# Laying the two blocks of a tile of query rows on alternate partitions instead of in halves

## The chip, the cores and the metric

The kernel runs on one core of one Trainium2 chip. The metric is the device time of one launch in microseconds. Three timed runs of the kernel before gave 817.63, 816.74 and 815.66 us: a median of 816.74 us. One further execution was profiled; everything that is read from the trace below comes from that one. The changed kernel computes the same output; only the place of rows in the on-chip memory and the order in which the host packs the query rows differ.

## The reference

Three layers run one after the other: attention with a position bias, a two-layer network, and a soft mixture of 8 experts.

```python
# attention: batch 4, 8 heads, 576 positions, 64 wide
scores = q @ k.T / 8
x    = log1p(|i - j|) / log1p(max(i, 1))         # i: query row, j: key row
bias = relu(x[..., None] @ w1 + b1) @ w2         # one 576 x 576 table per head
attn = softmax(scores + bias);  y = attn @ v     # -> 2304 tokens x 512
# network
h = y @ w_in                                     # 512 -> 2048
y = (max(h, 0) + alpha * min(h, 0)) @ w_out
# soft mixture: 32 slots, 4 for each of 8 experts
d = softmax(y @ phi, axis=0);  c = softmax(y @ phi, axis=1)
slots = d.T @ y
out   = c @ [relu(slots_e @ w1_e) @ w2_e  for each expert e]
```

The bias depends on the position and the head, not on the batch. So the kernel makes the bias table once, keeps it in device memory, and reads it back for each pair of heads.

## The kernel before, in words

**Blocks and tiles of query rows.** The 576 query rows are nine blocks of 64. Eight of them are paired to four tiles of 128 rows: tile c holds block c and block 8 - c, for c from 0 to 3. Block 4 is alone. In the kernel before, a tile's first block lies on partitions 0 to 63 and its second on partitions 64 to 127. The list `ROWS` on the host (L1281) says in which order the rows are packed, `_constants` (L1284) gives the positions of the rows of each tile in the same order, and `kernel` puts the output rows back into place with it (L1373).

**The bias phase (`bias_phase`, the first 77 us).** For nine groups k of 16 steps it makes step masks on ScalarE and VectorE (L142, L144), multiplies them on TensorE into sums `acc` (L160), and combines these on VectorE to bias rows (`tmp` L189, `rows` L193, L191), for the four tiles and for block 4. GpSimd writes the same values a second time, reversed, beside the first (L211), so that a row of the table holds the bias for all distances. When some columns of a tile are complete, `flush` sends them to device memory by `put` (L220), which calls `send` (L215): one DMA for the first block of the tile (`half` 0) and one for the second (`half` 1), each from 64 partitions (`q`, L222) to the tensor `W`, or to `W4` for block 4. Typical is one store of 64 rows x 4 head pairs x 1024 bytes, 256 KB. For head pairs 1 to 3 some stores are put off to the end of the phase (`late`).

**Attention (`Attention`).** It goes through 16 pairs of a head pair `hp` and a batch `b`, four batches to each head pair. For a head pair, the tile `nb` holds the bias of all its query rows. `bias_rows` (L324) fills it from `W` and `W4`: for each of the four 128-row tiles one read for the first block and one for the second, each of 64 rows into 64 partitions. For head pair 0 these are issued tile by tile (`bias_first`, L347), 288 KB a read, as early as the stores allow; for head pairs 1 to 3 all four tiles go in one read of 1152 KB a block, with two reads of 144 KB for block 4 (L345). For each pair and each of nine tiles: `scores` makes `s` on TensorE (L414), `least` subtracts the bias and takes the row's extreme on VectorE (`z`, `m`, L437), `power` takes the exponential on ScalarE (`e`, L457), `transposes` and `gather` turn it (`t` L477, `g` L491 and L493), and `pv` multiplies with the values (`o`, L505 and L510). Before the scores of a pair, GpSimd splits its inputs `raw` into high and low parts (`qh`, `kh` L382; `ql`, `kl` L384).

**What sets the order.** All DMAs around the change are issued by SyncE's queue, in program order from the late part of the bias phase on (`keep_in_program_order`). They go round eight completion semaphores: a DMA waits until the DMA issued eight before it has landed. In attention, the list `ROUND` (L299) fixes the order of the steps on the engines, with the scores of the next pair begun before the last pair is done. GpSimd also prepares inputs `x` of the network while attention runs (`xu` L634), from attention results that were stored to device memory (`xT` L518, `rs` L533 and L534) and read back (`xu` L619, `xb` L623). The network follows (`h` L725, `ys` L753), and then the experts (`hps` and `ops` L1136), with two steps around their start that the prediction names: `turn` (L1114), which a copy turns into `sst` (L1106 on ScalarE, L1108 on VectorE), and `tc` (L932), which turns the combine weights `cs` for the output.

Of the kernel before, what the change touches and what calls it, by code (L numbers as in the profile page):

```python
# [19 lines left out]
P = 128  # L20
B, H, S, D = 4, 8, 576, 64
# [48 lines left out]
def bias_phase(tc, ident, W, W4, cpack, lcol, prow, xmain, xtail, att):  # L70
# [3 lines left out]
    with ExitStack() as ctx:  # L74
# [73 lines left out]
        def unit(k, c):  # L148
# [4 lines left out]
            if c < 4:  # L153
                m, cols, dst = P, slice(P * c, P * c + P), acc
            else:
                m, cols = 64 * (k % 2) + 64, slice(512, S)
                dst = acc[m - 64 : m]
# [44 lines left out]
            a = both[:m, :, :, w + one - f0 - 64 : w + one - f0 - z]  # L202
            if c == 4:
                a, src = a[:, :, 0], fwd[:, :, 0]
# [10 lines left out]
            def send(dst, src, pin):  # L215
                i = nc.sync.dma_start(dst, src)
                if pin:
                    tc.keep_in_program_order(i)

            def put(half, blk, d0, n_r, n_l, one, hs):  # L220

                q = slice(64 * half, 64 * half + 64)  # L222
                if blk == 4:
                    e, dst = 1, W4.rearrange("h p j -> p h j")
                else:
                    e = 2
                    dst = W[blk - (blk > 4) if blk > 4 else 3 - blk, hs].rearrange("a p j b -> p a (j b)")
                src = mine.rearrange("p (h x) -> p h x", h=H // e)[:, hs if e == 2 else slice(0, H)]

                def move(j0, x0, n):  # L230
                    send(dst[:, :, e * j0 : e * (j0 + n)], src[q, :, e * x0 : e * (x0 + n)], k > 4)

                if one:
                    move(S - n_l, w - n_l + 1, n_l + n_r - 1)
                    return
                if n_r > 0:
                    move(S - 1 + d0, w, n_r)
                if n_l > 0:
                    y = int(d0 == 0)
                    move(S - d0 - n_l, w - n_l, n_l - y)  # L240

            def flush(hs):
                if c == 4:
                    for half in range(m // 64):
                        put(half, 4, d0 + 64 * half, 64, 64, False, hs)
                else:
                    far, near = min(w, S - 64 * c - d0), max(0, min(w, 64 * c + 64 - d0))
                    put(0, c, d0, far, near, one, hs)
                    put(1, 8 - c, d0, near, far, one, hs)
# [38 lines left out]
class Attention:  # L288
# [35 lines left out]
    def bias_rows(self, hp, s, n):  # L324

        nb = self.nb[hp]
        if s == 4:
            parts = [(64 * par, 4) for par in range(2)]
        else:
            parts = [(64 * q, s + 5 * q) for q in range(2)]  # L330
        for p0, blk in parts:
            i0 = 64 * (blk if blk >= 4 else 3 - blk)
            if s == 4:
                a = self.W4[2 * hp + p0 // 64, :, S - 1 - i0 : 2 * S - 1 - i0]
                src = bass.AP(tensor=a.tensor, offset=a.offset, ap=[[PITCH - 1, 64], [1, S]])
                dst = nb[p0 : p0 + 64, 8 * S :]
            else:
                a = self.W[blk - (blk > 4), hp, :, S - 1 - i0 : 2 * S - 1 - i0]
                step = H * 64 * PITCH + (128 if blk < 4 else -128)
                dims = [[2 * (PITCH - 1), 64], [step, n], [1, 2 * S]]  # L340
                src = bass.AP(tensor=a.tensor, offset=a.offset, ap=[d for d in dims if d[1] > 1])
                dst = nb[p0 : p0 + 64, 2 * S * s : 2 * S * (s + n)]
                if n > 1:
                    dst = dst.rearrange("p (s x) -> p s x", s=n)
            i = self.nc.sync.dma_start(dst, src)  # L345
            if hp == 0:
                self.tc.keep_in_program_order(i)  # L347
# [930 lines left out]

ROWS = [64 * blk + r for blk in (3, 5, 2, 6, 1, 7, 0, 8, 4) for r in range(64)]  # L1281


def _constants():  # L1284
    import numpy as np

    pos = np.arange(S)
    ld = np.log1p(pos.astype(np.float32))
    pi = np.log1p(np.maximum(pos.astype(np.float32), 1.0))
    x = (ld[None, :] / pi[:, None]).astype(np.float32)  # L1290
    lcol = np.repeat(ld.reshape(NTQ, 4).T, HID, axis=0)
    tiles = [np.r_[64 * c : 64 * c + 64, 64 * (8 - c) : 64 * (8 - c) + 64] for c in range(4)]
    up = (1 + np.maximum(pos, 1)).astype(np.float16)
    prow = np.tile(up[np.concatenate(tiles + [np.arange(256, 320)])][None, :], (P, 1))
    xmain = np.stack([x[r].reshape(P, NG, 64) for r in tiles], axis=2)
    mid = x[256:320]
    xtail = np.zeros((P, 3, 64), np.float32)
    for q in range(3):
        xtail[:64, q] = mid[:, 128 * q : 128 * q + 64]
        if q < 2:  # L1300
            xtail[64:, q] = mid[:, 128 * q + 64 : 128 * q + 128]

    row = np.arange(P).reshape(4, 2, 4, SPE)
    scon = np.zeros((P, P + 1), np.float32)
    for a in range(4):
        scon[row[:, :, 0], row[:, :, a]] = 1.0
    scon[row[:, :, 1::2].ravel(), P] = -1.0
    return dict(lcol=lcol, prow=prow, xmain=xmain, xtail=xtail, scon=scon)


def _layout(i):
    import numpy as np

    q = i["q"][:, :, ROWS].reshape(B, HP, 2, S, D).transpose(1, 0, 4, 2, 3)
    k = i["k"].reshape(B, HP, 2, S, D).transpose(1, 0, 4, 2, 3)
# [59 lines left out]
```

## Time and profile before

| | |
|---|---|
| median of three timed runs | 816.74 us (815.66 to 817.63) |
| the profiled execution: its own time | 816.62 us |
| the profiled execution: span of its instructions | 814.7 us |
| mean granted TensorE clock | 0.978 of full |
| TensorE matmul busy | 762.4 us (94%) |
| VectorE / ScalarE / GpSimd busy | 549.3 / 495.9 / 315.8 us |
| device memory read / written | 91.95 MB / 21.29 MB |

The span is what the trace covers; the execution's own time holds 1.9 us more around it. TensorE is the busy engine on the whole, but not in each stage: the bias phase and the start of attention have idle stretches of TensorE. [...]

### The profile page before, as it was taken

Reading aid. Unit: us, or ns where it says so; the run is one execution under the profiler, and the core shown is the slowest. Engines: PE = TensorE matmul, PEld = TensorE weight load, DVE = VectorE, ACT = ScalarE, POOL = GpSimd, SP = SyncE. Lnnn points to the kernel's source line nnn. Section 1 sums busy time; section 2 is a strip of 40 time slices with the busy share of each in tenths; the row PEclk is TensorE's granted clock in tenths of the full one; section 3 lists DMA queues with packets and bytes.
Section 4 is the critical chain, followed back from the end, with each engine's and each line's share of the span. In section 5 each row is a group of like instructions: output and inputs, shape, how many; then the busy total and the mean of one; then the engine's idle time right before and its main releaser. Section 6 shows DMA issues by size and latency. Waiting matters only on the chain.

```text
span 814.7 us, 18357 instructions
## 1 busy us (share of the span) xinstructions
PE 762.4 (94%) x7428; PEld 636.9 (78%) x7428; DVE 549.3 (67%) x958; ACT 495.9 (61%) x974; POOL 315.8 (39%) x239
## 2 busy tenths in 40 slices
PE   6886798999999999999999999999999999998993
PEld 6776676787877778988898989888888899886341
DVE  8887686888888856777778555655675756465103
ACT  8972787888888854444356566656566556655002
POOL 4633147275575713113224454445543641141000
PEclk9999799999999999999999999999999999999997
DMA  6598996748744542333340001401100124338996
GB/s 198 131 234 189 303 229 188 211 128 246 220 140 143 157 125 94 123 136 104 104 130 1 1 30 36 142 1 40 39 1 20 39 92 139 107 104 312 385 365 232
DMA packets 49670, 114.43 MB, mean 140 GB/s; under 512 B 10546, under 2 KB 29874, under 8 KB 47538
## 3 DMA queue, kind: packets, MB, share of 16 engines
q1 hardware_dynamic: 49584, 113.26, 44.7%
q8 instruction: 58, 0.95, 0.5%
q14 instruction: 28, 0.21, 0.1%
HBM read 91.95 MB, written 21.29 MB: 139 GB/s over the span
## 4 chain that ended last, share of the span: by engine, by line
PE 45%; DVE 3%; ACT 1%; DMA 1%; POOL 1%; issue 1%; DVEq 0%; ACTq 0%
PE h L725 18%; PE ys L753 18%; PE ops L1136 2%; PE hps L1136 2%; PE lp L823 1%; DMA em<-in_mw_dram 1%; PE turn L1145 1%; DVE x L644 0%; DVE g L736 0%; PE sp L882 0%; PE sp L883 0%; DVE wr L685 0%; DVE gr L741 0%; PE tl L870 0%; POOL w12l L714 0%
## 5 line engine op out<-in xcount | busy, mean ns | idle before, releaser
L736 DVE SCALAR_TENSOR_TENSOR g<-g,nal 128x384 f32<-128x384 f32 x96 | 100.9, 1051 | 84.0 <-ACT g L735 83.6
L437 DVE CUSTOM_DVE_ANT_0 z<-s,nb 128x576 f32<-128x576 f32 x144 | 108.3, 755 | 22.9 <-PE s L414 12.0
L457 ACT ACTIVATE e<-z,m 128x576 f32<-128x576 f32 x144 | 109.9, 767 | 6.7 <-DVE m L437 6.7
L739 ACT ACTIVATE gr<-g 128x384 fp32r<-128x384 f32 x96 | 50.2, 523 | 86.8 <-DVE g L736 86.6
L493 ACT ACTIVATE g<-t 128x640 f32<-128x640 f32 x96 | 67.3, 703 | 34.1 <-PE t L477 30.1
L505 PE MATMUL o<-g,v 128*64 128x256 f32 (+1 forms) x640 | 86.1, 414 | 0.5 <-ACT g L493 0.5
L733 ACT ACTIVATE g<-h 128x384 f32<-128x384 f32 x96 | 46.9, 489 | 54.4 <-PE h L725 50.1
L741 DVE TENSOR_TENSOR gr<-g,gr 128x384 fp32r<-128x384 f32 x80 | 53.6, 670 | 33.2 <-ACT gr L739 33.2
L477 PE MATMUL t<-ident,e 64*128 64x64 f32 x1440 | 69.1, 225 | 4.8 <-DVE m L437 2.9
L160 PE MATMUL acc<-wp,mask 128*128 128x64 bf16 (+1 forms) x1680 | 57.3, 198 | 16.9 <-issue 6.5
L477 PEld LDWEIGHTS t<-ident,e 64*128 64x128 f32 x1440 | 66.7, 141 | 6.7 <-issue 4.2
L160 PEld LDWEIGHTS <-mask 128*128 128x128 bf16 (+1 forms) x1680 | 55.2, 103 | 18.9 <-issue 7.5
L414 PE MATMUL s<-kh,qh 64*128 64x288 f32 x320 | 62.1, 384 | 4.7 <-DVE m L437 3.9
L505 PEld LDWEIGHTS o<-g,v 128*64 128x64 f32 x640 | 43.7, 138 | 29.0 <-ACT g L493 1.0
L142 ACT ACTIVATE mask<-pr,wb 128x576 bf16<-128x576 f16 (+4 forms) x94 | 54.9, 671 | 8.3 <-PE acc L160 8.3
L414 PE MATMUL s<-kl,qh 64*128 64x288 f32 x320 | 48.6, 299 | 2.6 <-POOL kl L384 2.6
L741 POOL TENSOR_TENSOR gr<-g,gr 128x384 fp32r<-128x384 f32 x16 | 19.4, 1212 | 77.7 <-issue 28.2
L414 PE MATMUL s<-kh,ql 64*128 64x288 f32 x320 | 48.6, 299 | 0.0
L382 POOL TENSOR_SCALAR qh<-raw 128x1216 fp32r<-128x1216 f32 x16 | 19.4, 1210 | 70.7 <-DMA raw<-in_qk_dram 49.5
L735 ACT ACTIVATE g<-h 128x384 f32<-128x384 f32 x96 | 46.5, 484 | 0.0
L384 POOL TENSOR_TENSOR ql<-raw,qh 128x1216 fp32r<-128x1216 f32 x16 | 45.2, 2827 | 0.0
L414 PEld LDWEIGHTS s<-kh,qh 64*128 64x128 f32 x320 | 31.5, 192 | 13.5 <-DVE m L437 4.4
(990 smaller groups left out, 2016.1 us busy)
## 6 DMA issues: line engine op xcount, KB each, us to landing
wide<-in_w_dram SPq DMA_DIRECT2D x16, 1024.0 KB
ep<-in_mw_dram SPq DMA_DIRECT2D x29, 512.0 KB
raw<-in_qk_dram SPq DMA_DIRECT2D x16, 896.0 KB
nb<-W SPq DMA_DIRECT2D x6, 1152.0 KB
v<-in_v_l_dram SPq DMA_DIRECT2D x16, 320.0 KB
pre<-in_mw_dram SPq DMA_DIRECT2D x10, 512.0 KB
ex<-in_mw_dram SPq DMA_DIRECT2D x9, 512.0 KB
em<-in_mw_dram SPq DMA_DIRECT2D x8, 512.0 KB
```

The lines of the kernel that those rows point to most:

```text
L142: nc.scalar.activation(dst, pr[:, :n], AF.Sigmoid, bias=wb[:, t : t + 1], scale=BIG)
L160: nc.tensor.matmul(dst[:, u // 8, :, :, 4 * (u % 8) : 4 * (u % 8) + 4], mask[:, (16 * k + u) % RING, cols], wp[:, part], start=part == 0, ...
L414: nc.tensor.matmul(s[:, hf, :288], st["q", a][d, o : o + P], st["k", b][d, 288 * h : 288 * h + 288], start=n_ == 0, stop=n_ == len(seq) - 1,),
L437: self.nc.vector.tensor_tensor_reduce(out=z.rearrange("p (a b) -> p a b", a=2), in0=s[:, :, :288], in1=nb.rearrange("p (a b) -> p a b", a= ...
L457: self.nc.scalar.activation(e, z, AF.Exp, bias=m, scale=-1.0, accum_out=st["sum"][:, slot : slot + 1]),
L477: self.pin(i, nc.tensor.transpose(tp[:, r, 64 * c : 64 * c + 64], e[q, k0 : k0 + P], self.ident[q, q]))
L493: self.pin(i, nc.scalar.activation(dst, src, AF.Copy))
L505: nc.tensor.matmul(op[64 * h : 64 * h + 64, 0, :n], st["v"][:, h, c], g[:, h, c], start=c == 0, stop=c == 4),
L725: nc.tensor.matmul(h, w_[:, c * P : (c + 1) * P], x_[:, c], start=c == 0 and n_ == 0, stop=c == NC - 1 and n_ == 2,)
L736: nc.vector.scalar_tensor_tensor(g, neg, self.nal[:, f : f + 1], g, ALU.mult, ALU.add)
L741: eng.tensor_tensor(gl, g, gh.bitcast(F32), ALU.subtract)
L753: i = self.nc.tensor.matmul(self.ys[blk][t], g_[:, t * P : (t + 1) * P], w_[:, 512:], start=f == 0 and n_ == 0, stop=f == NF - 1 and n_ == 2,)
```

## The change

A tile's first block now lies on the even partitions and its second block on the odd ones. On the host, `ROWS` and the position lists take rows of the two blocks in turn. In the kernel, `put` and `bias_rows` address partitions `half, half + 2, ...` in steps of two (`slice(half, P, 2)`, `slice(q, P, 2)`) in place of 64 neighbouring ones. Block 4 keeps its halves, in stores and in reads. Each DMA still moves 64 rows with the same bytes from and to the same addresses in device memory.

```diff
             def put(half, blk, d0, n_r, n_l, one, hs):
-                q = slice(64 * half, 64 * half + 64)
+                q = slice(64 * half, 64 * half + 64) if blk == 4 else slice(half, P, 2)
...
         if s == 4:
-            parts = [(64 * par, 4) for par in range(2)]
+            parts = [(slice(64 * par, 64 * par + 64), 4) for par in range(2)]
         else:
-            parts = [(64 * q, s + 5 * q) for q in range(2)]
-        for p0, blk in parts:
+            parts = [(slice(q, P, 2), s + 5 * q) for q in range(2)]
+        for p, blk in parts:
...
-                dst = nb[p0 : p0 + 64, 8 * S :]
+                dst = nb[p, 8 * S :]
...
-                dst = nb[p0 : p0 + 64, 2 * S * s : 2 * S * (s + n)]
+                dst = nb[p, 2 * S * s : 2 * S * (s + n)]
...
-ROWS = [64 * blk + r for blk in (3, 5, 2, 6, 1, 7, 0, 8, 4) for r in range(64)]
+ROWS = [64 * blk + r for n in (3, 2, 1, 0) for r in range(64) for blk in (n, 8 - n)] + list(range(256, 320))
...
-    tiles = [np.r_[64 * c : 64 * c + 64, 64 * (8 - c) : 64 * (8 - c) + 64] for c in range(4)]
+    tiles = [ROWS[P * (3 - c) : P * (4 - c)] for c in range(4)]
```

The instructions of SyncE and GpSimd stand in the same order before and after. The program is laid out by a scheduler, and it moves a few steps at the start of the experts. On TensorE, behind the eight products `turn`, the products `tc` stood ahead of the first `hps`, and now stand among them (the tile names are those of the section on the kernel; `pre`, `ep` and `et` are expert weights):

```order
-L932 MATMUL tc_0_10783<-ident,cs_0_10780 128x128 x2
 L1136 MATMUL hps<-pre,sst 32x512 x10
 L1136 MATMUL hps<-ep_9926,sst 32x512 x2
 L1136 MATMUL hps<-ep_9959,sst 32x512 x2
-L1136 MATMUL hps<-ep_10016,sst 32x512 x2
-L932 MATMUL tc_2_10798<-ident,cs_2_10795 128x128
+L1136 MATMUL hps<-ep_10016,sst 32x512
+L932 MATMUL tc_0_10783<-ident,cs_0_10780 128x128 x2
+L1136 MATMUL hps<-ep_10016,sst 32x512
```

Two products of `tc` have moved behind fifteen of the products of `hps`. On ScalarE at the same place, one copy of `turn` to `sst` and one exponential `c` change places:

```order
 L915 ACTIVATE c_0_10684<-c_0_10684 128x64
+L1106 ACTIVATE sst<-turn_10765 128x16x4
 L915 ACTIVATE c_2_10697<-c_2_10697 128x32
-L1106 ACTIVATE sst<-turn_10765 128x16x4
```

The copy to `sst`, for which the first `hps` waits, now stands one instruction earlier.

## Rows read from the trace of the kernel before

**Rows 1.** Busy time by stretch, with the columns' names; five stretches of the span.
```profile
core 0: us, PE busy (x) PEld busy (x) DVE busy (x) ACT busy (x) POOL busy (x), PEclk, DMA share, GB/s
...
76.00:98.00 22.00, 13.51 (x149) 11.13 (x148) 11.10 (x29) 12.48 (x27) 0.67 (x1) 0.69 0.98 271
...
133.00:142.00 9.00, 6.44 (x80) 4.91 (x76) 4.84 (x12) 5.13 (x11) 8.97 (x6) 0.81 0.75 181
142.00:290.00 148.00, 147.87 (x2187) 117.11 (x2185) 128.26 (x304) 124.41 (x270) 82.60 (x63) 1.00 0.59 176
290.00:740.00 450.00, 444.88 (x2457) 392.14 (x2452) 291.40 (x373) 251.31 (x468) 167.04 (x97) 1.00 0.23 75
740.00:814.60 74.60, 56.28 (x376) 27.98 (x375) 19.53 (x50) 15.53 (x38) 2.64 (x5) 0.90 0.88 333
```

**Rows 2.** Waits of the engines from 76 to 98 us: total, times, longest.
```profile
DVE z L437 <- DMA nb<-W: 8.0, 3, 3.9
...
PE s L414 <- DVE m L437: 3.9, 1, 3.9
```

**Rows 3.** Instructions in order of time, 73 to 87 us: start, duration, wait.
```profile
73.62 3.60 SPq L345 DMA_DIRECT2D nb<-W  x4
...
79.85 0.76 DVE L437 CUSTOM_DVE_ANT_0 z<-s,nb 128x576 f32<-128x576 f32 x1 [3.85 <-DMA nb<-W]
...
84.11 0.76 DVE L437 CUSTOM_DVE_ANT_0 z<-s,nb 128x576 f32<-128x576 f32 x1 [2.81 <-DMA nb<-W]
...
86.89 0.76 DVE L437 CUSTOM_DVE_ANT_0 z<-s,nb 128x576 f32<-128x576 f32 x1 [1.34 <-DMA nb<-W]
```

**Rows 4.** Instructions in order of time, 96 to 137 us, on SyncE, GpSimd and TensorE.
```profile
96.39 2.79 SPq L345 DMA_DIRECT2D nb<-W  x4
...
118.38 0.24 SPq L533 DMA_DIRECT2D rs<-rt  x1
...
126.99 1.01 POOL L634 TENSOR_TENSOR xu<-xu,xb 128x384 f32<-128x384 f32 x1 [13.64 <-DMA rs<-rt]
...
136.09 0.40 PE L414 MATMUL s<-kl,qh 64*128 64x288 f32 x2 [2.56 <-POOL kl L384]
```

**Rows 5.** Waits of SyncE's queue from 98 to 142 us: total, times, longest.
```profile
SPq L533 <- DMA nb<-W: 5.5, 1, 5.5
SPq L534 <- DMA nb<-W: 4.9, 1, 4.9
```

**Rows 6.** Busy time by stretch: loads of 128 rows, then two 64-row reads.
```profile
191.00:196.00 5.00, 5.00 (x82) 3.98 (x78) 4.28 (x13) 4.53 (x11) 5.00 (x4) 1.00 1.01 397
198.00:202.00 4.00, 4.00 (x41) 2.32 (x41) 2.90 (x7) 3.59 (x10) 0.00 (x0) 1.00 1.01 208
202.00:203.00 1.00, 1.00 (x22) 1.00 (x22) 0.96 (x3) 0.20 (x1) 0.58 (x1) 1.00 1.03 233
203.00:208.00 5.00, 5.00 (x76) 3.93 (x74) 4.61 (x12) 4.83 (x11) 5.00 (x4) 1.00 1.02 210
```

**Rows 7.** Busy time by stretch: the start of attention.
```profile
76.00:80.00 4.00, 0.81 (x11) 0.49 (x8) 0.15 (x1) 0.00 (x0) 0.67 (x1) 0.93 0.95 238
80.00:93.00 13.00, 8.85 (x86) 7.84 (x88) 7.86 (x20) 8.67 (x19) 0.00 (x0) 0.50 0.98 265
```

**Rows 8.** Busy time by stretch: the stores of the bias phase.
```profile
33.00:62.00 29.00, 25.22 (x753) 24.12 (x750) 23.07 (x46) 23.34 (x42) 9.86 (x15) 0.96 0.93 224
62.00:69.00 7.00, 5.04 (x168) 4.87 (x166) 6.50 (x16) 4.37 (x13) 2.24 (x3) 1.00 0.96 196
69.00:71.50 2.50, 2.50 (x93) 2.50 (x89) 2.50 (x6) 0.00 (x0) 1.00 (x2) 1.00 0.96 261
71.50:73.50 2.00, 1.35 (x47) 1.23 (x44) 1.49 (x4) 0.00 (x0) 0.95 (x2) 1.00 0.23 58
```

**Rows 9.** TensorE in order of time, start of the experts.
```profile
755.61 0.67 PE L932 MATMUL tc<-ident,cs 128*128 128x128 f32 x2
...
756.21 3.57 PE L1136 MATMUL hps<-pre,sst 128*32 128x512 f32 x17
```

More of the change, by code (lines that the diff above doesn't have):

```diff
@@ L327, in bias_rows @@
         if s == 4:
-            parts = [(64 * par, 4) for par in range(2)]
+            parts = [(slice(64 * par, 64 * par + 64), 4) for par in range(2)]
         else:
-            parts = [(64 * q, s + 5 * q) for q in range(2)]
-        for p0, blk in parts:
+            parts = [(slice(q, P, 2), s + 5 * q) for q in range(2)]
+        for p, blk in parts:
             i0 = 64 * (blk if blk >= 4 else 3 - blk)
             if s == 4:
-                a = self.W4[2 * hp + p0 // 64, :, S - 1 - i0 : 2 * S - 1 - i0]
+                a = self.W4[2 * hp + p.start // 64, :, S - 1 - i0 : 2 * S - 1 - i0]
                 src = bass.AP(tensor=a.tensor, offset=a.offset, ap=[[PITCH - 1, 64], [1, S]])
-                dst = nb[p0 : p0 + 64, 8 * S :]
+                dst = nb[p, 8 * S :]
             else:
```

## The prediction

> **What bounds the kernel now.** I read the table of busy time by stretch first, since an average over 815 us says little here. In it [rows 1] the reader is to see that TensorE fills the later stages: 147.87 of 148 us from 142 to 290, 444.88 of 450 from there to 740, with the DMA engines at 0.59 and 0.23. No faster transfer of bias rows helps in those 598 us, and after 740 none are moved. What is gained or lost ahead of 142 us therefore shifts all that follows, nearly one to one. Ahead of it two stretches have an idle TensorE: from 76 to 98 us it is busy 13.51 of 22 us, at a mean granted clock of 0.69, and from 133 to 142 us 6.44 of 9, at 0.81.
>
> Then I read who waits in these two. From 76 to 98 us VectorE waits for `nb`, the bias rows, three times and 8.0 us in all; TensorE waits 3.9 us for VectorE behind that [rows 2]. The places are the first tile, its companion, and the next [rows 3]: the first four reads are issued from 73.62 us on, and the first bias step starts at 79.85 us after 3.85 us of waiting; the others wait 2.81 us at 84.11 and 1.34 us at 86.89. Meanwhile the clock is at its lower level, 0.50 from 80 to 93 us, after 0.81 us of TensorE work in the 4 us ahead [rows 7].
>
> The second stall is a chain [rows 4]. The four reads for head pair 1 are issued from 96.39 us on. SyncE then has to wait for them, since its DMAs go round eight semaphores: 4.9 and 5.5 us [rows 5], until 118.38 us, when a store of `rs` goes out. GpSimd waits 13.64 us for what follows from it, starts on `xu` at 126.99 us, and comes late with the low part `kl` for the scores; TensorE stands 2.56 us until 136.09 us.
>
> Last I looked at how fast these reads go [rows 6]. Loads into 128 partitions, from 191 to 196 us, run at 397 GB/s with the 16 engines busy at 1.01. The 64-row bias reads from 198 to 208 us run at 208 and 210 GB/s, and the engines are as busy, 1.01 and 1.02. So a DMA engine takes 1.9 times as long for a byte in a 64-row transfer: all are at work, and something they share is full. The one faster stretch among these reads is the passage from the first 1152 KB read to the second, 233 GB/s from 202 to 203 us: there some engines still write the lower half of the partitions and others already the upper.
>
> **The change part by part.** It adds no instruction and removes none; the stores and reads keep bytes and count. Its cost or gain is the rate of 64-row transfers, and where they are waited for. The trace shows no transfer to every second partition, so its rate is bounded by the nearest rows: 397 GB/s, if the sharing goes away, and 208 GB/s, if it stays. It may also fall below what a mixed stretch has now, which the stores bound (the slower rival).
>
> [...]
>
> I take the lower side of the middle. [...] That passage ran at 233 against 209 GB/s, 11% more. I take 11% off the time of bias transfers in both waits, the row it is nearest to, and keep 0% and 47% (1 - 208/397) for the range.
>
> *The start of attention.* VectorE's waits for `nb` total 8.0 us, and the reads run on top of one another from 73.62 to 86.89 us, 13.3 us. 11% of the first is 0.9, of the second 1.5 us. TensorE's work here follows these steps; I take 1.0 us gained. The time at the lower clock I leave as it is.
>
> *The stall at 133 us.* The two reads of 1152 KB take 2 x 1.18 MB / 209 GB/s = 11.3 us; 11% is 1.2 us, which reaches SyncE's second wait and through `rs`, `xu` and the split `kl` the stall. 2.56 us becomes 1.3 us. The reads also start about 1 us sooner, but so does the step of TensorE that waits, so this gives nothing more. The low clock that follows stays. Gained: 1.2 us. The next head pairs' reads (issued near 135 and 193 us) end while TensorE is full; no gain [rows 1].
>
> *The stores.* From 33 to 71.5 us the DMA engines are busy 0.93 to 0.96 [rows 8]; then they fall to 0.23 ahead of the first read at 73.62 us. The stores' queue is empty by the time that the first bias rows are asked for. Faster stores gain nothing at the first read, by that cover; the few steps of GpSimd that wait for a store free up a little, and I count nothing.
>
> *The start of the experts.* The two `tc` products took 0.67 us in a gap of TensorE ahead of the first `hps` at 756.21 us [rows 9]. They now run among the `hps`, where TensorE is busy without a gap, and cost up to that 0.67 us; the copy to `sst` that stands earlier on ScalarE can return at most the 0.60 us by which the first `hps` started behind the first `tc`. I take 0.2 us lost, with -0.6 and +0.7 as bounds.
>
> *Sum.* Against the profiled execution's own 816.62 us, which is 0.1 us below the median of 816.74: 816.62 - 1.0 - 1.2 + 0.2 = 814.6 us, or 0.25% less.
>
> **The rivals.**
>
> *The sharing goes away.* [...] Then a 2 x 288 KB read, 2.5 us at the 238 GB/s of 76 to 80 us, takes 1.6 at 377 (397 at a share of 0.95), and each of three waits loses 0.9: 2.7 us. Less idling may bring the higher clock back sooner: 8.85 us of TensorE work ran at 0.50 from 80 to 93 us [rows 7], and a third of it at full clock would save 1.5. The reads of head pair 1 take 6 us in place of 11.3, so the 2.56 us stall goes. The mean clock of 0.81 over 9 us means 3.4 us at the low level [rows 1], half of which, 1.7, comes back. Sum: 816.62 - 2.7 - 1.5 - 2.6 - 1.7 + 0.2 = 808.3 us.
>
> *It does nothing.* [...] Time: 816.62 + 0.2 = 816.8 us, 815.5 to 818 with what small shifts do.
>
> *The stores become slower, and the first read is late.* [...] The stores from 33 to 71.5 us move 29 us x 224 GB/s + 7 x 196 + 2.5 x 261, 8.5 MB, in 36 us of busy engines. At the slowest rate seen, 196/0.96 = 204 GB/s, they need 41.7 us: 5.6 more. Idle shares ahead of 73.62 us cover 2.0 us (0.07 of 29) and 1.5 us (0.77 of 2). It decides once the stores grow by more than 3.5 us; at 5.6 the first read, and all that follows, is 2.1 us later: 816.62 + 2.1 + 0.2 = 818.9 us. [...]
>
> **How the numbers follow.** My forecast of partial relief, 814.6 us, has a chance of 0.40, with its own range from 812.5 to 816.2; full relief 0.28, with 806.5 to 811; nothing 0.19; slower stores 0.13, with 818 to 821. A measurement of this kernel tells about 0.2% from no change, 1.6 us: faster is below 815.1 us, slower above 818.4. Faster takes full relief, 0.28, and about 0.65 of partial relief, 0.26: 0.54. Slower takes about 0.10 of the slow rival and 0.03 of unforeseen shifts in the other cases: 0.13. The rest is 0.33. The range from 806.8 to 818.6 us leaves out a little of the fastest and most of the slow rival, about 0.15. By bounds the unknown rate alone spans 808.3 to 816.8.
>
> **What would show it right or wrong.** In the profile of the changed kernel, the rate of the large bias reads tells the cases apart: stretches at a DMA share of 1.0 with little else in flight run near 230 GB/s by my forecast, near 390 by the first rival, at 210 by the second. VectorE's three waits for `nb` total about 7, 5 or 8 us. The first bias step starts about 0.5 us before 79.85 us by mine, 1 us or more before by the first rival, and past 81 us by the third, with no idle stretch of the DMA engines ahead of 73 us. TensorE's wait for `kl` near 133 us is about 1.3 us, gone, or still 2.6 us. The stretch from 142 us to the end should be as long as now within 1 us; if the time moves by more than what is gained or lost ahead of it, the shift itself has changed something further on, and my sum is wrong there.

## The result: slower by 0.7%, and where the time went

The changed kernel takes 821.89 us (median of 4 runs, 821.49 to 823.0) against 816.6 us for the kernel before (median of 4, 815.66 to 817.63). The ratio is 1.007, with an interval from 1.0054 to 1.0085. The forecast was 814.6 us in a range from 806.8 to 818.6, so the time rose where a fall was forecast, and it lies above the range. The profiled execution took 821.84 us, with a span of 819.9 us.

The busy time of the kernel after by stretch, with the edges of [rows 1] and one stretch more, from 98 to 133 us. Each engine has its busy time and, in brackets, its instructions; PEclk is the granted TensorE clock as a share of full speed, and DMA share the mean busy share of the 16 DMA engines.

```profile
core 0: us, PE busy (x) PEld busy (x) DVE busy (x) ACT busy (x) POOL busy (x), PEclk, DMA share, GB/s
...
76.00:98.00 22.00, 10.40 (x108) 9.37 (x108) 10.04 (x21) 9.51 (x21) 4.12 (x3) 0.53 0.98 342
98.00:133.00 35.00, 32.72 (x452) 25.09 (x452) 27.05 (x66) 26.35 (x57) 16.36 (x13) 0.95 0.40 135
133.00:142.00 9.00, 9.00 (x143) 7.28 (x139) 7.86 (x20) 7.48 (x18) 2.57 (x3) 1.00 0.41 132
142.00:290.00 148.00, 146.51 (x2131) 114.70 (x2129) 129.82 (x304) 124.16 (x272) 85.88 (x65) 1.00 0.55 183
290.00:740.00 450.00, 444.79 (x2514) 392.97 (x2513) 292.88 (x377) 252.64 (x472) 166.83 (x97) 1.00 0.22 73
```

In the kernel before, the stretch that [rows 1] leaves out was full:

```profile
98.00:133.00 35.00, 35.00 (x511) 27.29 (x508) 28.87 (x69) 29.04 (x65) 17.86 (x14) 1.00 0.85 237
```

TensorE has lost 3.11 us of busy time between 76 and 98 us and 2.28 between 98 and 133, and gained 2.56 between 133 and 142. From 142 to 290 us it loses 1.36 more, 1.2 of it in one wait near 237 us; the stretch behind that is as full as before. So most of the loss sits at the start of attention, where a gain was forecast. The granted clock went with it: it is 0.53 in the mean from 76 to 98 us, against 0.69 before, and 0.95 against 1.00 from 98 to 133.

The two waits there, in the kernel after, which answer to [rows 2] (total, times, longest):

```profile
PE s L414 <- DVE m L437: 13.7, 1, 13.7
DVE z L437 <- DMA W<-rows: 13.6, 1, 13.6
```

And the same place in order of time, to be read beside [rows 3]:

```profile
69.25 3.70 SPq L345 DMA_DIRECT2D nb<-W  x4
...
74.56 1.22 SPq L345 DMA_DIRECT2D nb<-W  x2
...
77.16 2.73 SPq L345 DMA_DIRECT2D nb<-W  x4
...
84.97 0.76 DVE L437 CUSTOM_DVE_ANT_0 z<-s,nb 128x576 f32<-128x576 f32 x1 [13.64 <-DMA W<-rows]
85.66 0.75 DVE L437 CUSTOM_DVE_ANT_0 z<-s,nb 128x576 f32<-128x576 f32 x1
```

The first reads of bias rows are issued 4.4 us sooner than before (69.25 against 73.62 us), and yet the first bias step starts 5.1 us later (84.97 against 79.85). It waits once, for 13.64 us; the companion and the next tiles then wait for no transfer. Before, there were three shorter waits, one for each slot of `nb`. The wait is labelled with the stores of `W`, but a wait for several semaphores is put down to the one that came last, and here stores were still being issued, eight of them from 79.93 us on. What the step really waits for stands in the program's own list of instructions with their waits. First the kernel before, then after; `z0_0` is the first bias step and `z0_2` the first that uses the second slot:

```
105 L437 ISA z0_0_2264,m0_0_2265<-s0_0_2257,nb0_2016 128x576 [waits DMAHW5_49,DMAHW6_49,PE_49,Activation_49]
109 L437 ISA z0_2_2286,m0_2_2287<-s0_2_2277,nb0_2016 128x576 [waits DMAHW4_49,DMAHW3_49,PE_49]

105 L437 ISA z0_0_2264,m0_0_2265<-s0_0_2257,nb0_2016 128x576 [waits DMAHW3_49,DMAHW4_49,DMAHW2_49,DMAHW5_49,DMAHW1_49,DMAHW6_49,DMAHW0_49,DMAHW7_49,PE_49,Activation_49]
109 L437 ISA z0_2_2286,m0_2_2287<-s0_2_2277,nb0_2016 128x576 [waits PE_49]
```

Before, the first step waits for two DMA lanes, the two reads of its own slot, and a later one for the next two. After, it waits for all eight lanes, which carry every read of head pair 0, and later steps wait for none. The lists read as if the framework that places the waits takes a write to every second partition of `nb` as touching all its columns, so that each step of the pair depends on each read. The dependency is false: the step uses the columns of one slot.

The new timing has a second cost. VectorE's short step `r`, behind the nine tiles of the first pair, took 0.17 us before and takes 2.59 after; it ends together with GpSimd's `ql`, which runs beside it. First the step before, then the two instructions after:

```profile
93.50 0.17 DVE L523 SCALAR_TENSOR_TENSOR r<-sum 128x9 f32<-128x9 f32 x1 [0.94 <-ACT e L457]
```

```profile
95.70 2.75 POOL L384 TENSOR_TENSOR ql<-raw,qh 128x1216 fp32r<-128x1216 f32 x1
95.89 2.59 DVE L523 SCALAR_TENSOR_TENSOR r<-sum 128x9 f32<-128x9 f32 x1 [0.94 <-ACT e L457]
```

The next bias step follows at 98.64 us, and TensorE waits 2.11 us for it, until 99.40. In the kernel before, `ql` started at 101.58 us, well behind `r`; after, it comes 5.9 us sooner and `r` 2.4 us later. Why `r` takes longer beside `ql` was not tested.

The transfers did become faster. The large reads of head pair 3, which answer to the 208 and 210 GB/s of [rows 6], and two stretches of stores, to be read beside [rows 8], in the kernel after:

```profile
198.00:204.00 6.00, 6.00 (x85) 4.32 (x81) 4.39 (x10) 5.51 (x13) 2.08 (x2) 1.00 1.01 382
...
33.00:62.00 29.00, 27.03 (x840) 25.65 (x836) 26.06 (x56) 25.77 (x49) 11.26 (x17) 1.00 0.97 272
62.00:69.00 7.00, 5.59 (x186) 5.37 (x183) 6.77 (x14) 1.39 (x4) 2.63 (x4) 1.00 0.34 107
```

Reads of 64 rows run at 382 GB/s, with the engines as busy (1.01) as at 208 before. Stores run at 272 GB/s from 33 to 62 us, against 224, and from 62 to 69 us the DMA engines are busy only 0.34, against 0.96: most stores have already gone.

By milestones, the kernel after is later by 5.1 us at the first bias step, by 3.8 at the last one (297.9 against 294.1), by 3.9 at the product `turn` ahead of the experts (757.61 against 753.72), and by 5.2 at the end (819.9 against 814.7).

### The profile page after: what moved, and what is told of

It reads as the page before. It is cut to its first block, busy times and chain, and to the rows that moved or that the text cites. A ratio compares the mean times of both kernels' runs of the same rounds, so it can differ in the third digit from the quotient of the medians.

```text
span 819.9 us, 18356 instructions
## 1 busy us (share of the span) xinstructions
PE 764.2 (93%) x7428; PEld 637.7 (78%) x7428; DVE 553.9 (68%) x958; ACT 495.3 (60%) x974; POOL 315.1 (38%) x239
## 4 chain that ended last, share of the span: by engine, by line
PE 45%; DVE 3%; ACT 1%; DMA 1%; POOL 1%; issue 0%; DVEq 0%; ACTq 0%
PE h L725 18%; PE ys L753 18%; PE ops L1136 2%; PE hps L1136 2%; PE lp L823 1%; DMA em<-in_mw_dram 1%; PE o L1163 1%; PE turn L1145 1%; DVE x L644 0%; DVE g L736 0%; PE sp L882 0%; PE sp L883 0%; DVE wr L685 0%; DVE gr L741 0%; PE tl L870 0%
```

## The experiments

Theory A: the new layout doubles the rate of 64-row transfers, and the loss is the first bias step's wait for all reads of head pair 0. Theory B: the faster stores crowd the queues and make the reads late. Theory C: transfers to every second partition cost something by themselves. Times are medians; each ratio is to the kernel before on the same chip (815.5 to 816.0 us there).

**One read of 128 rows for each slot of head pair 0 (whole_rows_read).** A slot's two blocks lie on alternate partitions, so both can come in one transfer over all 128, and nothing is written to every second partition of `nb` before the first step. The edit to the kernel after, in `bias_rows`:

```
+        elif hp == 0:
+            a = [self.W[blk, hp, :, S - 1 - i0 : 2 * S - 1 - i0] for blk, i0 in ((s, 64 * (3 - s)), (s + 4, 64 * (s + 5)))]
+            dims = [[2 * (PITCH - 1), 64], [a[1].offset - a[0].offset, 2], [1, 2 * S]]
+            src = bass.AP(tensor=a[0].tensor, offset=a[0].offset, ap=dims)
+            i = self.nc.sync.dma_start(nb[:, 2 * S * s : 2 * S * (s + 1)], src)
```

> The kernel after, but a slot's bias rows for head pair 0 come in one transfer over all 128 partitions instead of two over every second one, so that the first bias step waits only for the first slot (its list of waits holds one DMA lane instead of eight); the order of the engines' work is that of the kernel before, its tail too. Theory A (the loss is the first bias step's wait for all eight reads of head pair 0, plus a tail in another order): first z at 73 to 77 us (it was 84.97 after and 79.85 before), the stall near 133 gone as after, total 806 to 811. Theory B (the reads are late because the faster stores crowd the queues, whatever is waited for): first z stays at 83 to 86, total 819 to 821. Theory C (transfers or reads over every second partition cost the engines something all along): the first z is early but the total stays within 2 us of 816.6.

Measured: 809.27 us, ratio 0.992 (0.989 to 0.9949). Its reads and first steps in order of time:

```profile
70.83 1.27 SPq L333 DMA_DIRECT2D nb<-W  x1
...
76.58 0.76 DVE L444 CUSTOM_DVE_ANT_0 z<-s,nb 128x576 f32<-128x576 f32 x1 [3.42 <-DMA nb<-W]
...
80.14 0.76 DVE L444 CUSTOM_DVE_ANT_0 z<-s,nb 128x576 f32<-128x576 f32 x1 [2.11 <-DMA nb<-W]
```

The first step is at 76.58 us, and each slot again has a wait of its own. Theory A holds in both numbers. The profiled execution took 815.28 us, more than the other five (807.14 to 811.21), so its span isn't compared with those of other kernels.

**Stores alone in the new layout (stores_only), and reads alone (reads_only).** In the first, only the rows of the bias phase (`q` in `put`, and the host's lists of positions) alternate; in the second, only query rows and reads (`parts` in `bias_rows`, and `ROWS`).

```
stores_only, against after:
-            parts = [(slice(q, P, 2), s + 5 * q) for q in range(2)]
+            parts = [(slice(64 * q, 64 * q + 64), s + 5 * q) for q in range(2)]

reads_only, against after:
-                q = slice(64 * half, 64 * half + 64) if blk == 4 else slice(half, P, 2)
+                q = slice(64 * half, 64 * half + 64)
```

> Stores over every second partition as after; query rows and reads of bias rows in halves as before. Order of all engines as before, the first bias step waits for the first slot's two reads alone. Theory A: the stores run at about 297 GB/s in 33 to 50 us instead of 216, the first read is issued at about 69.3 instead of 73.62, and the reads stay near 208 GB/s; first z at 75 to 77, total 811 to 814, with the stall near 133 still there. Theory B (fast stores crowd the first read): first z at 83 to 86, total 819 to 822.

> Query rows and reads over every second partition as after, stores in halves as before. The first bias step waits for all eight reads of head pair 0 as after. Theory A: the store phase is as before (first read issued at about 73.6), the reads run at about 400 GB/s, first z at 84 to 88, tail in the order of after, no stall near 133; total 820 to 824. Theory B (the stores' form is what made the kernel slower): first z at 78 to 80, total 814 to 817.

Measured: 813.45 us for the stores alone, ratio 0.9975 (0.9953 to 0.9997), and 821.02 us for the reads alone, 1.006 (1.0036 to 1.0084). First the kernel with stores alone, then that with reads alone; in each the first read's issue and the first bias step:

```profile
71.29 2.50 SPq L345 DMA_DIRECT2D nb<-W  x4
...
76.74 0.76 DVE L437 CUSTOM_DVE_ANT_0 z<-s,nb 128x576 f32<-128x576 f32 x1 [3.99 <-DMA nb<-W]
```

```profile
73.30 2.51 SPq L345 DMA_DIRECT2D nb<-W  x4
...
87.80 0.76 DVE L437 CUSTOM_DVE_ANT_0 z<-s,nb 128x576 f32<-128x576 f32 x1 [12.97 <-DMA W<-rows]
```

And a stretch of stores and one of the large reads of head pair 3, in the same order:

```profile
33.00:50.00 17.00, 15.65 (x480) 15.12 (x477) 12.39 (x27) 17.00 (x29) 5.96 (x9) 0.97 0.97 307
...
192.00:204.00 12.00, 12.00 (x173) 9.25 (x173) 9.85 (x24) 10.05 (x24) 7.13 (x5) 1.00 1.02 212
```

```profile
33.00:50.00 17.00, 15.22 (x468) 14.45 (x465) 13.25 (x28) 17.00 (x28) 5.99 (x9) 1.00 0.91 215
...
198.00:204.00 6.00, 6.00 (x88) 4.32 (x83) 4.50 (x12) 5.62 (x13) 2.19 (x2) 1.00 1.01 387
```

Each layout sets the rate of its own transfers: stores at 307 beside reads at 212 GB/s, and 215 beside 387. Fast stores with an early first step refute theory B; slow stores with the late step and the full loss refute it again. Two details of what was expected did not come: the first read was issued at 71.29, not 69.3 us, and the stall near 133 us was gone although these reads are as slow as before.

**The wait alone, in the layout of before (halves_with_the_wait).**

```
+        if i == 0 and t == 0:
+            for n in (1, 2, 3):
+                w = self.zp.tile([P, 1], F32, tag="hold", name=f"hold{n}", bufs=1)
+                self.nc.vector.tensor_copy(w, nb[:, 2 * S * n : 2 * S * n + 1])
+                self.nc.vector.tensor_copy(m, w)
```

> The kernel before, all in halves, with six copies of one element on VectorE that read slots 1, 2 and 3 of head pair 0's bias ahead of the first bias step, so that it waits for all of them as after does. Theory A: first z at 87 to 90 us (before 79.85), the tail in the order of after, total 821 to 826, so that the wait alone makes this kernel slower without any change of layout. Theories B and C: the wait is a minor thing, the bias steps catch up within head pair 0, total 816 to 818.

Measured: 825.44 us, ratio 1.0094 (1.0061 to 1.0128). VectorE's wait for the reads, and the first bias step:

```profile
DVE hold L434 <- DMA nb<-W: 12.7, 3, 8.2
```

```profile
87.94 0.76 DVE L442 CUSTOM_DVE_ANT_0 z<-s,nb 128x576 f32<-128x576 f32 x1 [0.24 <-DVE m L435]
```

With no change of layout, the wait for all slots moves the first step by 8.1 us and the median by 9.9 (7.7 by the ratio, with 5.0 to 10.4 as its interval). That is enough to account for the changed kernel's loss of 5.3 us, even if the new layout by itself gains some us.

**Which transfers alternate (first_slot_strided, other_slots_strided).** Both are the kernel with whole reads, but one keeps two alternate reads for slot 0, the slot of the first step, and the other keeps them for slots 1 to 3. The first step's list of waits holds two DMA lanes in the one and seven in the other.

```
first_slot_strided:  -        elif hp == 0:    +        elif hp == 0 and s > 0:
other_slots_strided: -        elif hp == 0:    +        elif hp == 0 and s == 0:
```

> The kernel after with slots 1, 2 and 3 of head pair 0 read in one whole transfer each; slot 0, the one that the first bias step uses, is still read by two transfers over every second partition. The first step's list of waits holds the two lanes of slot 0 alone. Theory A (the loss is the wait for all eight reads, which every write to alternate partitions draws in): first z at 75 to 77 us, total 807 to 812. If reads over every second partition are themselves late to land: first z at 83 to 86 and total 818 to 822, since the two reads that the first step needs are those of after.

> The converse: slot 0 in one whole transfer, slots 1, 2 and 3 by two transfers each over every second partition. The first step's list of waits holds seven lanes again, and the tail is in the order of after. Theory A: first z at 83 to 86 us, total 818 to 823, although the transfer that the first step needs is the whole one. If such reads are themselves late: first z at 75 to 77 (its own read is whole), total 807 to 813.

Measured: 809.46 us, ratio 0.9917 (0.9885 to 0.9949), where slot 0 alternates, and 820.15 us, 1.0044 (1.0027 to 1.0061), where the others do. In this order, the first read's issue and the first bias step:

```profile
69.26 2.51 SPq L352 DMA_DIRECT2D nb<-W  x4
...
73.87 0.76 DVE L444 CUSTOM_DVE_ANT_0 z<-s,nb 128x576 f32<-128x576 f32 x1 [2.89 <-DMA nb<-W]
```

```profile
68.44 0.57 SPq L333 DMA_DIRECT2D nb<-W  x1
...
82.94 0.76 DVE L444 CUSTOM_DVE_ANT_0 z<-s,nb 128x576 f32<-128x576 f32 x1 [12.80 <-DMA W<-rows]
```

This pair settles it. The first step is early though its own reads alternate, and late though its own read is a whole one: what counts is whether the *other* slots are written to every second partition. The two differ by 10.7 us. That is what the false wait costs in the new layout, with all that comes with it: a long `r` (2.55 us) and the new order of steps at the experts. Theory C falls with it. The early step came even 1 us sooner than expected.

**Whole reads for every head pair (all_reads_whole).** In `bias_rows`, the branch for head pair 0 is taken for all, once per slot.

> Alternate partitions as after, with one transfer over 128 partitions per slot for every head pair instead of for head pair 0 alone: no write to every second partition of the bias rows is left. Theory A (nothing is lost by such reads once nothing waits for them): as with head pair 0's whole reads alone, first z at 75.5 to 77, total 807 to 811, and the median within 2 us of 809.3. If reads over every second partition still cost something later (contention, a wait for all of a pair's rows): 2 to 6 us less.

Measured: 810.38 us, ratio 0.9923 (0.9896 to 0.995), with the first step at 76.16 us. Within the intervals of 0.3% it does not differ from the version for head pair 0 alone, so no cost of alternate reads shows where nobody waits for them.

**Whole reads in the layout of before (halves_whole_reads).** Here partition order demands that the block be the outer dimension of the source, of size 2:

```
+            dims = [[a[1].offset - a[0].offset, 2], [2 * (PITCH - 1), 64], [1, 2 * S]]
```

> The kernel before, all in halves, but a slot's bias rows for head pair 0 come in one transfer over all 128 partitions. Stores as before, order of the engines' work and tail as before. If what is left of the gain after the wait is mended comes from the stores: first read issued at about 73.5, first z at 79 to 80, the third at 82 to 83.5 (84.11 before), total 814 to 816. If the reads of head pair 0 carry it: first z below 78, total 808 to 812, near the kernel with alternate partitions and whole reads.

Measured: 848.53 us, ratio 1.0378 (1.0342 to 1.0413), which neither expectation allowed for. The first steps of four slots and a stretch between them:

```profile
85.27 0.76 DVE L444 CUSTOM_DVE_ANT_0 z<-s,nb 128x576 f32<-128x576 f32 x1 [12.09 <-DMA nb<-W]
...
97.48 0.76 DVE L444 CUSTOM_DVE_ANT_0 z<-s,nb 128x576 f32<-128x576 f32 x1 [10.77 <-DMA nb<-W]
...
109.00 0.76 DVE L444 CUSTOM_DVE_ANT_0 z<-s,nb 128x576 f32<-128x576 f32 x1 [10.08 <-DMA nb<-W]
...
120.90 0.76 DVE L444 CUSTOM_DVE_ANT_0 z<-s,nb 128x576 f32<-128x576 f32 x1 [9.04 <-DMA nb<-W]
```

```profile
92.00:94.00 2.00, 0.00 (x0) 0.00 (x0) 0.00 (x0) 0.00 (x0) 0.00 (x0) 0.50 0.13 53
```

The 16 DMA engines are busy 0.13 in the mean, as much as 2 of them at work throughout, and move 53 GB/s. A read of 128 x 1152 x 4 bytes, 590 KB, takes 11.1 us at that rate, about the length of each wait; together they are 42.0 us. The run was meant to tell the share of the reads from that of the stores, and does not; beyond the 2 us of the stores alone, that split stays open. The same bytes, with 64 as the outer dimension in whole_rows_read and 2 here, are waited for at most 3.42 us there, and 9.04 to 12.09 us here.

## Why the prediction was wrong

**What bounds the kernel: right.** Beyond 142 us little gives the shift back: TensorE's busy time from 290 to 740 us is 444.79 us after and 444.88 before [rows 1], and the later milestones move by 3.8 to 5.2 us.

**The start of attention: the step that failed.** It took the three waits of [rows 2, 3] as they stood, one read behind another, and shortened them by 11%, a gain of 1.0 us. It spoke of the lengths of the waits and never asked whether the changed write would still be waited for slot by slot. It also misread the three places, as the first tile, its companion and the next: they are the first tiles of three slots, and a companion (at 80.53 us) waits for no read. In place of three waits that shrink there was one for every read, and the first step moved by +5.1 us. The other kernels price this: 9.9 us for the wait alone in the old layout, and 10.7 between the pair that differs in which slots alternate. The time at the lower clock, which the forecast left as it was, grew: the clock is 0.50 from 80 to 93 us in both kernels, but from 93 to 98 us it is 0.52 after, against 0.99 before. None of the rivals has this single wait: the slower one expected a late *issue* of the first read, and that came 4.4 us early. The list of waits told it without a run: its two rows stand above.

**The rate: the wrong side of the middle.** The forecast took 11% off the time of bias transfers, the step from 209 to 233 GB/s at the passage between the two large reads [rows 6]. That the new layout would run at the rate of this passage was the author's estimate, and no run shows it: the trace has 382 GB/s, with 208 before at the same share of 1.01. So the rate that the rival "the sharing goes away" took, near 397 GB/s, nearly came. That something the engines share is full in a 64-row transfer was the author's inference from 208 against 397 GB/s; the runs show the rate of each layout, not its cause. That rival's sum, 808.3 us, is close to the 809.27, 809.46 and 810.38 us of the three kernels without the false wait, but this is in part luck. The rival has 2.7 us from shorter waits for `nb` and nothing from the stores; in the first two of these kernels the waits fell only from 8.0 to 6.8 us, and the first read is issued 2.8 and 4.4 us sooner. Most of their reads for head pair 0 are whole ones, too, which the rival does not have.

**The stall at 133 us: gone, but not for the reason given.** TensorE is busy 9.00 of 9 us there. The term gave 1.2 of 2.56 us, from faster reads. But the wait for `kl` [rows 4] is also gone where the large reads still run at 212 GB/s (stores alone) and in the old layout with the added wait. In these two the reads of head pair 1 are issued at 92.57 and 94.10 us, against 96.39, and the load of GpSimd's `xu` at 116.40 and 120.06, against 122.04; in the second, TensorE's own steps also come later, by 8.1 us at the first bias step. An earlier start goes with the end of the stall at the old rate, so the stall says nothing on the rate. What faster reads alone would have done to it was not measured.

**The stores: worth about 2 us, not 0.** Alone they bring 0.25%, with 0.03 to 0.47% as the interval. The argument was that their queue is empty ahead of 73.62 us [rows 8]. The DMA engines are indeed at 0.23 there, but that is beside the point: the phase as a whole ended sooner. The first read is issued between 68.44 and 71.66 us in the six kernels with alternate stores, 70.1 in the mean, and between 70.95 and 73.62 in the four with stores in halves, 72.7 in the mean. Which wait inside the phase grew shorter stays open. GpSimd's own wait for stores fell only from 4.0 to 3.2 us:

```profile
POOL rows L211 <- DMA W<-rows: 4.0, 2, 2.4
```

```profile
POOL rows L211 <- DMA W<-rows: 3.2, 2, 2.1
```

(before, then after).

**The start of the experts: about right.** The term was +0.2 us. From `turn` to the end of the span the kernel before takes 61.0 us and after 62.3, but this varies from run to run. The six profiled kernels with the order of before take 61.0 to 62.1 us, 61.7 in the mean, and the four with the order of after 60.8 to 62.5, 62.0 in the mean. The new order of `tc` goes with the false wait (halves_with_the_wait has it, whole_rows_read does not). The 1.3 us more of the one pair can't be told from that spread.

## What to carry to other kernels

When a change alters which partitions or columns a transfer writes, compare the waits that each reader carries before any rate is weighed: a tile written in pieces is only read piece by piece as long as the dependency tracking can tell the pieces apart. A single wait that replaces several, at the first reader, is its mark in a trace, and the name of its releaser can mislead. Here the kernel gains 0.8%, at 809.3 us, as soon as each slot comes in one transfer over all 128 partitions.

## What the runs showed of the hardware that was not expected

Sixty-four rows on alternate partitions move nearly at the 397 GB/s of 128-row loads [rows 6]: 382 to 387 GB/s at a DMA share of 1.01, against 208 to 212 on 64 neighbouring ones. And the transfer whose source has an outer dimension of 2 kept the 16 DMA engines busy only 0.13 in the mean, at 53 GB/s. How its packets were spread over the engines no run shows.
